# Gathers of the third expert behind the second one's weights, fetches spread over five experts, the fallback as one loop

## The chip, the cores and the metric

The kernel runs on one core of a Trainium2 chip. The metric is device time in microseconds, lower is better. TensorE (PE in the rows) multiplies, VectorE (DVE) and ScalarE (ACT) move and split the results, GpSimd (POOL) splits weights and issues the indirect DMAs, SyncE (SP) issues most of the other DMAs.

## What is computed

A linear attention over 4 x 768 positions gives 3072 tokens of 256 numbers. They pass a first mixture of experts, where each token goes to the one expert of eight that its gate chooses, and then a second one of four experts that all tokens pass.

```python
logits = x @ w_gate                          # 3072 tokens, 8 experts
expert_idx = np.argmax(logits, axis=1)
...
for e in range(E):
    mask = expert_idx == e
    if not mask.any():
        continue
    xe = x[mask]
    h = np.maximum(xe @ w1[e], 0.0)          # 256 x 1024
    ye = h @ w2[e]                           # 1024 x 256
    out[mask] = gate_w[mask, None] * ye
...
for e in range(E):                           # second stage, 4 experts
    h = np.maximum(x @ w1[e], 0.0)
    out += p[:, e:e + 1] * (h @ w2[e])
```

## The kernel before

Numbers of 32 bits are multiplied as three products of halves: a high part (hh, xh, wh) and the rest (hl, xl, wl). ACT makes the high part by a cast, VectorE or POOL the rest by a subtraction.

The attention takes the time up to about 113 us, the eight experts of the first stage stand from there to 288, the second stage from 292 to the end. The eight experts go by their size, each with a fixed number of token places (CAPS: 472, 488, 456, 424, 416, 400, 384, 376). A token over the capacity of its expert would be left for the **fallback**, a block that runs only if `left > 0`; with these inputs it is not run. "Expert 0" below is the first one in this order.

An expert e has these parts, on all engines in the order that is written here:

- **gathers** (`gather_turn`, L265): up to four indirect DMAs on POOL fetch its tokens, 128 rows each, from `xs` in DRAM into `xg`, of which there are eight buffers. An expert's gathers are issued some experts ahead.
- **make_x**: TensorE transposes the rows (tpx, L278), ACT and VectorE split them into xh and xl (L281, L282).
- **gemm1x**: eight blocks f of 128 hidden units. Each takes six products (L248) into ph, which has three buffers; ACT takes the relu as hh (L838), VectorE the rest as hl (L840). So the products of block f + 3 wait for hl of block f. After each block a `hook` adds small steps from a list to the engines' orders.
- **gemm2x**: two times 24 products (L859) and a copy into x2 (L864).
- **prep(e + 1)**: loads of the next expert's weights (512 KB each, SP, L132), their cast wh on ACT (L146), and wl on POOL for w1 (L152) or on VectorE for w2 (L150). In the names, wl_3_0 is the first half for expert 3.

Expert 0 has a part of 256 places that starts under the attention, and a second part of 216 places, whose eight blocks stand from 126 to 140 us.

The list that the hook works off, `queue`, holds the bookkeeping of the first stage: four `turn_steps` (small vectors of 8 numbers, among them `over` with L941 to L946), `places` (pl on POOL, place on VectorE), `weights2`, ten steps of `invert` (VectorE: t, ot, ot times tokc, m and six one-hot tables om; TensorE: ip), the store of 3072 places of 4 bytes into `idd`, one each to its own address (L994), and then 24 times `fetch(u)`, an indirect DMA on POOL that reads the second stage's weights of 128 tokens (pgs from pgd, L1002). A fetch is issued behind the last split of weights on POOL.

TensorE, VectorE, ACT and POOL keep the order that is written; a wait of one instruction holds what stands behind it on its engine.

Of the kernel before, what the change touches and what calls it, by code (L numbers as in the profile page):

```python
# [19 lines left out]
P = 128  # L20
# [15 lines left out]
NSL = 512  # L36
NC = E1 * NSL // P + 1
BIG = 3 << 29
OUTSIDE = 16384


def body(tc, I, out):
    nc = tc.nc
    with ExitStack() as outer:
# [5 lines left out]
        xs = dp.tile([NT, D], F32, name="xs")  # L50
        pgd = dp.tile([NT, E2], F32, name="pgd")
        idd = dp.tile([NT + P, 1], I32, name="idd")
        zero = cp.tile([P, 1], I32, name="zero")
        nc.vector.memset(zero, 0)

# [813 lines left out]
        with ExitStack() as ctx:  # L869
# [88 lines left out]
            def gather_turn(e):  # L958
                gather(e, range(tiles(e)), xs, idr.rearrange("p e c -> p (e c)"), 4 * (e - STAY))
# [52 lines left out]
            for e in range(E1):  # L1012
                if e == E1 - 2:
                    operands = x_first()

                def hook(f, e=e):
                    if operands:
                        operands.pop(0)()
                    if queue and e and (e > 1 or len(queue) > NQ):
                        queue.pop(0)()  # L1020
                    if f % 4 == 3:
                        prep(e + 1, f // 4)
                    if e == 0 and f in (4, 6):
# [12 lines left out]
                if e == 0:  # L1036
                    gemm2x(0, hs, CAP0, CAPS[0], bass.ds(BASES[0], CAPS[0] - CAP0), lambda k: prep(1, 2 + k))
                else:
                    gemm2x(e, hs, 0, CAPS[e], bass.ds(BASES[e], CAPS[e]), lambda k: prep(e + 1, 2 + k))


            left = nc.values_load(tab[0:1, 3, 0:1], min_val=0, max_val=NT)
            with tc.If(left > 0, preferred_fallthrough_block=False), tc.tile_pool(name="fall", bufs=1) as fp:
                starts = nc.values_load_multi_w_load_instructions(tab[0:1, 1, :], min_val=0, max_val=NT)[1]
                turns = nc.values_load_multi_w_load_instructions(tab[0:1, 4, :], min_val=0, max_val=E1 - 1)[1]
                ends = nc.values_load_multi_w_load_instructions(tab[0:1, 2, :], min_val=0, max_val=NT)[1]
                for e in range(E1):
                    w1, w2 = (I[k][bass.ds(turns[e], 1)].rearrange("o r c -> (o r) c") for k in ("w1", "w2"))
                    with tc.For_i(starts[e], ends[e], P) as ws:
                        ix = fp.tile([P, 1], I32, name="ixf")  # L1050
                        nc.sync.dma_start(ix, idd[bass.ds(ws, P)])
                        xg = m1.tile([P, D], F32, tag="xg", name="xgf", bufs=8)
                        nc.gpsimd.indirect_dma_start(xg, None, xs, bass.IndirectOffsetOnAxis(ap=ix, axis=0))
                        xT = m1.tile([P, 2, P], F32, tag="xg", name="xTf", bufs=8)
                        tp = pm.tile([P, 2, P], F32, tag="oneC", name="tpf", bufs=2)
                        for k in range(2):
                            nc.tensor.transpose(tp[:, k, :], xg[:, k * P:k * P + P], ident)
                        nc.scalar.copy(xT, tp)
                        hf = fp.tile([P, NF, P], F32, tag="hf", name="hf")
                        for j in range(2):  # L1060
                            raw = [mp.tile([P, 512], F32, tag="hh", name="raw0f", bufs=10) for _ in range(2)]
                            for k in range(2):
                                nc.sync.dma_start(raw[k], w1[k * P:k * P + P, j * 512:j * 512 + 512])
                            for f in range(4):
                                ph = pm.tile([P, P], F32, tag="three", name="phf", bufs=3)
                                for k in range(2):
                                    nc.tensor.matmul(ph, raw[k][:, f * P:f * P + P], xT[:, k, :],
                                                     start=(k == 0), stop=(k == 1))
                                nc.scalar.activation(hf[:, 4 * j + f, :], ph, AF.Relu)
                        raws = []  # L1070
                        for j in range(4):
                            raw = mp.tile([P, 2, D], F32, tag="hl", name="raw1f", bufs=10)
                            nc.sync.dma_start(
                                raw, w2.rearrange("(k p) d -> p k d", p=P)[:, j * 2:j * 2 + 2, :])
                            raws.append(raw)
                        for k in range(2):
                            po = pm.tile([P, P], F32, tag="two", name="pof", bufs=2)
                            for f in range(NF):
                                nc.tensor.matmul(po, raws[f // 2][:, f % 2, k * P:k * P + P], hf[:, f, :],
                                                 start=(f == 0), stop=(f == NF - 1))  # L1080
                            dst = bass.ds(ws, P)
                            (nc.vector.tensor_copy if k else nc.scalar.copy)(x2[k][:, dst], po)
                x_again()

        m1s.close()
# [199 lines left out]
```

## Time and profile before

| | |
|---|---|
| median of 3 runs | 824.31 us (822.92 to 825.62) |
| the profiled execution | 822.34 us, of which its span 820.6 us |
| TensorE | busy 773.1 us (94% of the span), mean granted clock 0.969 |
| VectorE | busy 580.1 us (71%) |
| ScalarE | busy 406.2 us (49%) |
| GpSimd | busy 480.2 us (59%) |

The span is the profiled execution from its first instruction to its last, and its own time is a little longer than it. A row of the timeline has the start in us, the duration, the engine and line, what is written from what, the shape, and in brackets the idle time of the engine before it and what ended it. A clock of 1.00 is the full 2.4 GHz, 0.50 the lower level of 1.2 GHz.

### The profile page before, as it was taken

What the parts mean: (1) busy time and instruction counts of PE and PEld (TensorE: products, weight loads), DVE (VectorE), ACT (ScalarE), POOL (GpSimd) and SP (SyncE); (2) the same over time, 40 slices, a digit from 0 to 9 for tenths busy, and PEclk for the clock granted to TensorE, in tenths of its full rate; (3) what the DMA queues carried; (4) which work ended last, traced back from release to release, by engine and by line L of the source; (5) the groups of instructions that cost most, each with busy time, mean ns of one, the idle gap of its engine ahead of it and who ended that gap; (6) DMA issues with size and microseconds to landing.
All of it is one profiled execution on the core that took longest, in us unless ns stands there. A gap on an engine that the chain in (4) does not pass through costs nothing.

```text
span 820.6 us, 16313 instructions
## 1 busy us (share of the span) xinstructions
PE 773.1 (94%) x6296; PEld 728.4 (89%) x6296; DVE 580.1 (71%) x1050; ACT 406.2 (49%) x858; POOL 480.2 (59%) x538
## 2 busy tenths in 40 slices
PE   8879987899999969999999999999999999999994
PEld 5556577789999969999999999999999999999994
DVE  8697882665445656776887777978767877778853
ACT  5533343434455445455555455565554655554540
POOL 5546645624588065356876355977435886465634
PEclk8998997999999979999999999999999999999998
DMA  8943225433843310000000000100000000000001
GB/s 220 226 124 97 64 42 178 151 109 104 122 124 118 91 30 26 2 1 27 26 27 27 1 2 1 52 27 26 2 2 1 26 27 1 1 27 28 26 27 52
DMA packets 41688, 46.41 MB, mean 57 GB/s; under 512 B 10432, under 2 KB 30656, under 8 KB 41600
## 3 DMA queue, kind: packets, MB, share of 16 engines
q1 hardware_dynamic: 37040, 37.09, 16.9%
q0 software_dynamic: 3360, 7.13, 2.9%
q8 instruction: 51, 0.84, 0.4%
q10 hardware_dynamic: 1200, 1.05, 0.4%
q14 instruction: 37, 0.30, 0.1%
HBM read 38.90 MB, written 6.35 MB: 55 GB/s over the span
## 4 chain that ended last, share of the span: by engine, by line
PE 60%; issue 1%; POOL 1%; ACT 1%; DVE 0%; POOLq 0%; ACTq 0%
PE po L1174 32%; PE x L1113 9%; PE z L1113 8%; PE w L1113 8%; PE y L1113 4%; POOL out L1194 1%; ACT s L1126 0%; ACT xc L802 0%; PE poA L1174 0%; POOLq L1281 0%; POOL g L1131 0%; ACT wh L178 0%; POOL gap L1199 0%; DVE h L1122 0%; DVE c L1148 0%
## 5 line engine op out<-in xcount | busy, mean ns | idle before, releaser
L1174 PE MATMUL po<-w,h 128*128 128x256 f32 x2280 | 281.4, 281 | 0.3 <-DVE h L1122 0.3
L1174 PEld LDWEIGHTS po<-w,h 128*128 128x128 f32 x2280 | 279.0, 189 | 0.5 <-DVE h L1122 0.5
L1119 ACT ACTIVATE h<-c 128x384 fp32r<-128x384 f32 x192 | 98.8, 525 | 150.2 <-DVE c L1148 84.8
L1122 DVE SCALAR_TENSOR_TENSOR h<-c,h 128x384 fp32r<-128x384 f32 x192 | 150.2, 791 | 11.3
L1131 POOL TENSOR_TENSOR g<-s,s 128x384 f32<-128x384 f32 x64 | 65.1, 1017 | 145.7 <-ACT s L1130 145.7
L1133 DVE TENSOR_TENSOR u<-y,s 128x384 f32<-128x384 f32 x64 | 35.5, 555 | 75.2 <-ACT s L1130 70.1
L1113 PE MATMUL x<-xc,wh 128*128 128x384 f32 x256 | 67.4, 345 | 7.5 <-issue 4.1
L803 POOL TENSOR_TENSOR xc<-x,xc 128x384 fp32r<-128x384 f32 x32 | 36.5, 1140 | 51.0 <-ACT xc L802 50.7
L1113 PE MATMUL w<-xc,wh 128*128 128x384 f32 x256 | 66.2, 340 | 0.0
L1113 PE MATMUL z<-xc,wh 128*128 128x384 f32 x256 | 66.1, 340 | 0.0
L838 ACT ACTIVATE hh<-ph 128x216 fp32r<-128x216 f32 (+8 forms) x68 | 33.5, 495 | 57.5 <-PE ph L248 38.4
L248 PE MATMUL ph<-xh,wh 128*128 128x488 f32 (+8 forms) x142 | 51.2, 361 | 10.0 <-DVE hl L840 7.7
L1148 DVE TENSOR_TENSOR c<-u,g 128x384 f32<-128x384 f32 x64 | 60.4, 944 | 0.0
L840 DVE SCALAR_TENSOR_TENSOR hl<-ph,hh 128x216 fp32r<-128x216 f32 (+8 forms) x68 | 37.5, 557 | 28.1 <-ACT hh L838 22.1
L1126 ACT COPY s<-x 128x384 f32<-128x384 f32 x64 | 30.7, 480 | 53.4 <-PE x L1113 53.4
L152 POOL TENSOR_TENSOR wl<-raw,wh 128x1024 fp32r<-128x1024 f32 (+1 forms) x22 | 39.6, 1800 | 26.8 <-ACT wh L146 25.0
L1122 DVE SCALAR_TENSOR_TENSOR h<-x,h 128x384 fp32r<-128x384 f32 x64 | 35.7, 558 | 24.8 <-ACT h L1119 24.5
L803 POOL TENSOR_TENSOR xc<-ts,xc 128x384 fp32r<-128x384 f32 x46 | 52.4, 1153 | 0.0
L1113 PEld LDWEIGHTS x<-xc,wh 128*128 128x128 f32 x256 | 42.6, 190 | 11.0 <-ACT s L1126 6.1
L501 POOL TENSOR_TENSOR Sm<-S,smask 128x256 f32<-128x256 f32 x44 | 31.3, 729 | 35.9 <-DVE S L491 29.1
L248 PE MATMUL ph<-xh,wl 128*128 128x488 f32 (+8 forms) x142 | 50.3, 354 | 0.3 <-POOL wl L152 0.3
L248 PE MATMUL ph<-xl,wh 128*128 128x488 f32 (+8 forms) x142 | 50.1, 353 | 0.0
(236 smaller groups left out, 1743.9 us busy)
## 6 DMA issues: line engine op xcount, KB each, us to landing
raw<-in_w SPq DMA_DIRECT2D x30, 512.0 KB
raw<-in_v SPq DMA_DIRECT2D x32, 256.0 KB
xs<-xo SPq DMA_DIRECT2D x24, 128.0 KB
xz<-in_xt SPq DMA_DIRECT2D x6, 384.0 KB
CT<-in_CT SPq DMA_DIRECT2D x7, 192.0 KB
BT<-in_BT SPq DMA_DIRECT2D x7, 192.0 KB
bt<-in_bt SPq DMA_DIRECT2D x3, 384.0 KB
ar<-in_ar SPq DMA_DIRECT2D x3, 384.0 KB
```

Source lines behind the costliest of these rows:

```text
L152: ins = nc.gpsimd.tensor_sub(lo[:, :, a:a + n], raw[:, :, a:a + n], hi[:, :, a:a + n].bitcast(F32))
L248: mm = nc.tensor.matmul(ph, w[:, k, fs], x[k], start=(i == 0), stop=(i == 5))
L803: eng.tensor_sub(o[:, 1], src, o[:, 0].bitcast(F32))
L838: i0 = nc.scalar.activation(hh, ph, AF.Relu)
L840: i1 = nc.vector.scalar_tensor_tensor(hl, ph, 0.0, hh.bitcast(F32), op0=ALU.max, op1=ALU.subtract)
L1113: nc.tensor.matmul(bank[to], w[:, a], x[:, r], start=(m == 0 and to not in seen), stop=(m == 2), skip_group_check=True)
L1119: sc.activation(HP[n][0], src, AF.Relu)
L1122: v.scalar_tensor_tensor(HP[n][1], src, 0.0, HP[n][0].bitcast(F32), op0=ALU.max, op1=ALU.subtract)
L1131: nc.gpsimd.tensor_add(g_, s5, s7)
L1133: v.tensor_add(u2, bank["y"], s1)
L1148: v.tensor_add(c22, u2, g_)
L1174: nc.tensor.matmul(two[h], x[:, ts], w2[:, w, j], start=(i, j, h * (len(hs) - 1), m) == (0, 0, 0, 0), stop=(i, j, m) == (3, 1, 2), skip_gr ...
```

## The change

It has three parts. First, the four gathers of the third expert (e = 2) are no longer issued behind the blocks of expert 0, but behind its gemm2x, after the last split of expert 1's first weights on POOL. Second, the list is worked off at every block from expert 1 on, one step for each, where before only four steps ran in expert 1; behind every third fetch stands an empty step. Third, the fallback, which was eight loops behind each other, one for each expert, becomes one loop over a list of parts of 128 tokens; the list is worked out inside the block. The block is also no longer told which of its sides is to follow the branch directly.

```diff
 NSL = 512
 NC = E1 * NSL // P + 1
 BIG = 3 << 29
+NLIST = NU + E1
 OUTSIDE = 16384
...
 
-            NQ = NU + NU // 4 + 6
             queue = turn_steps + [places, weights2] + [f for f in invert(
                 rt, place, 0, NU, NU, placed, lambda sh, name: pp.tile(sh, F32, tag="oneA", name=name), 1) if f]
-            queue += [lambda u=u: fetch(u) for u in range(NU)]
+
+            queue += [f for u in range(NU) for f in [lambda u=u: fetch(u)] + [lambda: None] * (u % 3 == 2)]
...
                 def hook(f, e=e):
                     if operands:
                         operands.pop(0)()
-                    if queue and e and (e > 1 or len(queue) > NQ):
+                    if queue and e:
                         queue.pop(0)()
                     if f % 4 == 3:
                         prep(e + 1, f // 4)
...
                 X.pop(e)
-                if e + 2 < E1:
+                if 0 < e < E1 - 2:
                     gather_turn(e + 2)
...
                 if e == 0:
                     gemm2x(0, hs, CAP0, CAPS[0], bass.ds(BASES[0], CAPS[0] - CAP0), lambda k: prep(1, 2 + k))
+                    with tc.issue_after(LOW[0]):
+                        gather_turn(2)
                 else:
                     gemm2x(e, hs, 0, CAPS[e], bass.ds(BASES[e], CAPS[e]), lambda k: prep(e + 1, 2 + k))
 
 
             left = nc.values_load(tab[0:1, 3, 0:1], min_val=0, max_val=NT)
-            with tc.If(left > 0, preferred_fallthrough_block=False), tc.tile_pool(name="fall", bufs=1) as fp:
-                starts = nc.values_load_multi_w_load_instructions(tab[0:1, 1, :], min_val=0, max_val=NT)[1]
...
-                for e in range(E1):
-                    w1, w2 = (I[k][bass.ds(turns[e], 1)].rearrange("o r c -> (o r) c") for k in ("w1", "w2"))
-                    with tc.For_i(starts[e], ends[e], P) as ws:
-                        ix = fp.tile([P, 1], I32, name="ixf")
-                        nc.sync.dma_start(ix, idd[bass.ds(ws, P)])
-                        xg = m1.tile([P, D], F32, tag="xg", name="xgf", bufs=8)
-                        nc.gpsimd.indirect_dma_start(xg, None, xs, bass.IndirectOffsetOnAxis(ap=ix, axis=0))
...
+            with tc.If(left > 0), tc.tile_pool(name="fall", bufs=1) as fp:
+
+                def t8(name, shape, dt=F32):
+                    return fp.tile([P, *shape], dt, name=name)
+
+                st, n, ni, pc, lt = t8("st", (E1,)), t8("n", (E1,)), t8("ni", (E1,), I32), t8("pc", (E1,)), t8("lt", (E1, E1))
+                v.tensor_copy(st, tab[:, 1])
+                v.tensor_copy(n, tab[:, 2])
+                v.tensor_sub(n, n, st)
...
+                parts_ = nc.values_load(all_[0:1, 0:1], min_val=0, max_val=NLIST)
+                with tc.For_i(0, parts_, 1) as part:
+                    cell = fp.tile([1, 2], I32, name="cell")
+                    nc.sync.dma_start(cell, lid[bass.ds(part, 1)])
+                    ws = nc.values_load(cell[0:1, 0:1], engines=(mybir.EngineType.SP, mybir.EngineType.Activation,
+                                                                 mybir.EngineType.DVE), min_val=0, max_val=NT)
+                    turn = nc.values_load(cell[0:1, 1:2], engines=(mybir.EngineType.SP,), min_val=0, max_val=E1 - 1)
+                    w1, w2 = (I[k][bass.ds(turn, 1)].rearrange("o r c -> (o r) c") for k in ("w1", "w2"))
+                    ix = fp.tile([P, 1], I32, name="ixf")
+                    nc.sync.dma_start(ix, idd[bass.ds(ws, P)])
...
```

Inside the new block some 25 small VectorE steps work out the list, and the loop's body is that of one of the old loops.

**POOL, from the gathers of experts 1 and 2 on.** The rows go to the first half of expert 2's weights (xg are gathers, pl belongs to `places`). Before:

```order
L265 DMA xg<-xs,idr 128x256 x8
L152 TENSOR_TENSOR wl_1_0_2423<-raw_1_0_2302,wh_1_0_2422 128x1024
L265 DMA xg<-xs,idr 128x256 x2
L152 TENSOR_TENSOR wl_1_1_2467<-raw_1_1_2304,wh_1_1_2466 128x1024
L265 DMA xg<-xs,idr 128x256 x2
L988 TENSOR_TENSOR pl<-oneh,base 128x192
L265 DMA xg<-xs,idr 128x256 x2
L152 TENSOR_TENSOR wl_2_0_2696<-raw_2_0_2693,wh_2_0_2695 128x1024
L265 DMA xg<-xs,idr 128x256 x2
L152 TENSOR_TENSOR wl_2_1_2738<-raw_2_1_2735,wh_2_1_2737 128x1024
```

After:

```order
L267 DMA xg<-xs,idr 128x256 x4
L154 TENSOR_TENSOR wl_1_0_2424<-raw_1_0_2303,wh_1_0_2423 128x1024
L154 TENSOR_TENSOR wl_1_1_2468<-raw_1_1_2305,wh_1_1_2467 128x1024
L267 DMA xg<-xs,idr 128x256 x8
L990 TENSOR_TENSOR pl<-oneh,base 128x192
L267 DMA xg<-xs,idr 128x256 x2
L154 TENSOR_TENSOR wl_2_0_2697<-raw_2_0_2694,wh_2_0_2696 128x1024
L267 DMA xg<-xs,idr 128x256 x2
L154 TENSOR_TENSOR wl_2_1_2747<-raw_2_1_2744,wh_2_1_2746 128x1024
```

Four of the first eight gathers move behind wl_1_1, and the split wl_1_1 stands directly behind wl_1_0; ahead of pl there are now eight gathers.

**VectorE in the blocks of expert 2** (456 places; hl is the rest of a block, all other rows come from the list). Before:

```order
L840 SCALAR_TENSOR_TENSOR hl<-ph,hh 128x456
L989 TENSOR_REDUCE place<-pl 128x24
L990 TENSOR_TENSOR place<-place,rank 128x24
L840 SCALAR_TENSOR_TENSOR hl<-ph,hh 128x456 x2
L227 TENSOR_SCALAR t<-place 128x24
L840 SCALAR_TENSOR_TENSOR hl<-ph,hh 128x456
L217 TENSOR_TENSOR ot<-iota_76,t 128x576
L218 TENSOR_TENSOR ot<-ot,tokc 128x576
L840 SCALAR_TENSOR_TENSOR hl<-ph,hh 128x456
L228 SCALAR_TENSOR_TENSOR m<-t,place 128x24
L840 SCALAR_TENSOR_TENSOR hl<-ph,hh 128x456
L213 TENSOR_TENSOR om<-iota_74,m 128x512
```

After:

```order
L842 SCALAR_TENSOR_TENSOR hl<-ph,hh 128x456
L230 SCALAR_TENSOR_TENSOR m<-t,place 128x24
L842 SCALAR_TENSOR_TENSOR hl<-ph,hh 128x456
L215 TENSOR_TENSOR om<-iota_75,m 128x512
L842 SCALAR_TENSOR_TENSOR hl<-ph,hh 128x456
L215 TENSOR_TENSOR om<-iota_75,m 128x512
L842 SCALAR_TENSOR_TENSOR hl<-ph,hh 128x456
L215 TENSOR_TENSOR om<-iota_75,m 128x512
L842 SCALAR_TENSOR_TENSOR hl<-ph,hh 128x456
L215 TENSOR_TENSOR om<-iota_75,m 128x512
L842 SCALAR_TENSOR_TENSOR hl<-ph,hh 128x456
L215 TENSOR_TENSOR om<-iota_75,m 128x512
```

The steps place, t, ot and ot times tokc are gone from here; they stand in the blocks of expert 1, ot times tokc behind its last xl. From the second block on there is one om behind each hl, six in all.

**TensorE at the branch around the fallback** (the branch of L1043 before, of L1047 after). Before, from the branch through the loop of the first expert:

```order
L1043 COMPARE_AND_BRANCH
L1043 UNCONDITIONAL_BRANCH
L1044 TENSOR_LOAD tab
L1046 TENSOR_LOAD tab
L1049 COMPARE_AND_BRANCH
L1049 UNCONDITIONAL_BRANCH x2
L1281 BRANCH_PREFETCH_HINT
L1057 MATMUL tpf<-ident,xgf 128x128 x2
L1067 MATMUL phf<-xTf,raw0f 128x128 x16
L1079 MATMUL pof<-hf,raw1f 128x128 x16
L1049 REGISTER_ALU
L1049 COMPARE_AND_BRANCH
```

After, the whole block:

```order
L1047 COMPARE_AND_BRANCH
L1087 TENSOR_LOAD all__4053
L1088 COMPARE_AND_BRANCH
L1088 UNCONDITIONAL_BRANCH x2
L1326 BRANCH_PREFETCH_HINT
L1102 MATMUL tpf<-ident,xgf 128x128 x2
L1112 MATMUL phf<-xTf,raw0f 128x128 x16
L1124 MATMUL pof<-hf,raw1f 128x128 x16
L1088 REGISTER_ALU
L1088 COMPARE_AND_BRANCH
L1088 UNCONDITIONAL_BRANCH
L1047 UNCONDITIONAL_BRANCH x2
```

Before, the branch falls through to an unconditional branch that leads over eight loops like this one. After, the branch leads to the last of the rows, which leads on to the row behind it; one loop lies between. The other engines have the same two layouts.

The store into idd moves on SP as well: before it stands behind all four loads for expert 4, after behind the first of them.

## Rows read from the trace of the kernel before

**Rows 1.** Windows: us, busy of five engines, TensorE clock, DMA share, GB/s.
```profile
129.00:135.00 6.00, 1.67 (x7) 1.41 (x7) 0.76 (x2) 0.82 (x3) 3.23 (x4) 0.67 0.84 275
...
135.00:141.00 6.00, 6.00 (x28) 6.00 (x29) 1.99 (x6) 3.02 (x8) 2.38 (x1) 0.50 0.43 111
...
292.00:296.00 4.00, 4.00 (x16) 4.00 (x17) 2.49 (x5) 2.58 (x6) 1.57 (x2) 0.65 0.02 6
...
325.00:800.00 475.00, 474.40 (x3395) 471.84 (x3394) 364.11 (x596) 257.93 (x541) 288.75 (x291) 1.00 0.05 17
```

**Rows 2.** Timeline of TensorE: gaps in the first stage, transposes of expert 2.
```profile
131.41 0.55 PE L248 MATMUL ph<-xh,wh 128*128 128x216 f32 x1 [2.96 <-DVE hl L840]
...
134.94 0.55 PE L248 MATMUL ph<-xh,wh 128*128 128x216 f32 x1 [1.92 <-DVE hl L840]
...
153.55 0.82 PE L278 MATMUL tpx<-ident,xg 128*128 128x128 f32 x6
...
159.60 0.49 PE L248 MATMUL ph<-xh,wh 128*128 128x488 f32 x1 [1.92 <-DVE tab L943]
...
182.31 0.48 PE L248 MATMUL ph<-xh,wh 128*128 128x456 f32 x1 [1.65 <-DVE hl L840]
...
218.95 0.46 PE L248 MATMUL ph<-xh,wh 128*128 128x416 f32 x1 [0.63 <-DVE hl L840]
...
291.96 1.01 PE L1113 MATMUL x<-xc,wh 128*128 128x384 f32 x2 [4.12 <-issue]
```

**Rows 3.** Branch records (ns min/median/max), VectorE behind it, instruction queue 284 to 297 us.
```profile
L1043 PEldq COMPARE_BRANCH  x2: 95/1892/3690, 285.2 to 288.2; - x2
...
291.90 0.56 DVE L793 TENSOR_TENSOR ts<-x,x 128x384 f32<-128x384 f32 x1 [3.47 <-issue]
...
q14 instruction: 7, 0.06, 1.3%
```

**Rows 4.** Timeline of POOL: gathers of expert 2, splits of weights.
```profile
128.46 0.95 POOL L265 DMA_INDIRECT xg<-xs,idr  x1 [0.30 <-issue]
...
132.21 0.94 POOL L265 DMA_INDIRECT xg<-xs,idr  x1 [0.30 <-issue]
...
143.55 2.40 POOL L152 TENSOR_TENSOR wl<-raw,wh 128x1024 fp32r<-128x1024 f32 x1
...
156.56 2.38 POOL L152 TENSOR_TENSOR wl<-raw,wh 128x1024 fp32r<-128x1024 f32 x1
...
178.54 2.55 POOL L152 TENSOR_TENSOR wl<-raw,wh 128x1024 fp32r<-128x1024 f32 x1 [12.32 <-ACT wh L146]
```

**Rows 5.** Timeline of VectorE: two long steps, one om.
```profile
156.56 2.42 DVE L944 TENSOR_SCALAR nov<-nov 128x8 f32<-128x8 f32 x1
...
178.89 2.82 DVE L218 TENSOR_TENSOR ot<-ot,tokc 128x576 f16<-128x576 f16 x1
...
182.81 0.68 DVE L213 TENSOR_TENSOR om<-iota,m 128x512 f16<-128x512 f16 x1
```

**Rows 6.** Timeline of SP's queue: load of expert 4, store, load of expert 5.
```profile
190.43 0.37 SPq L132 DMA_DIRECT2D raw<-in_w  x1
...
200.82 0.39 SPq L994 DMA_DIRECT2D idd<-idc  x1
...
203.29 0.37 SPq L132 DMA_DIRECT2D raw<-in_w  x1
```

**Rows 7.** Timeline of ACT: relus of expert 0, casts, a copy.
```profile
130.59 0.35 ACT L838 ACTIVATE hh<-ph 128x216 fp32r<-128x216 f32 x1 [5.28 <-remote]
...
134.12 0.35 ACT L838 ACTIVATE hh<-ph 128x216 fp32r<-128x216 f32 x1 [3.18 <-issue]
...
205.20 1.04 ACT L146 CAST wh<-raw 128x1024 fp32r<-128x1024 f32 x1
...
214.03 0.52 ACT L864 COPY x<-po 128x424 f32 x1 [6.82 <-remote]
...
220.82 1.05 ACT L146 CAST wh<-raw 128x1024 fp32r<-128x1024 f32 x1
```

More of the change, by code (lines that the diff above doesn't have):

```diff
@@ L52, in body @@
         idd = dp.tile([NT + P, 1], I32, name="idd")
+        lid = dp.tile([NLIST, 2], I32, name="lid")
         zero = cp.tile([P, 1], I32, name="zero")
@@ new lines, in body, with wide @@
+            with tc.If(left > 0), tc.tile_pool(name="fall", bufs=1) as fp:
[5 more added lines that the diff above has]
+                v.tensor_sub(n, n, st)
+                v.tensor_scalar(n, n, 127.0, None, op0=ALU.add)
+                v.tensor_copy(ni, n)
+                v.tensor_scalar(ni, ni, 7, None, op0=ALU.logical_shift_right)
+                v.tensor_copy(n, ni)
+                v.tensor_tensor(lt, rows(nth), cols(nth), op=ALU.is_lt)
+                v.tensor_mul(lt, lt, rows(n))
+                v.tensor_reduce(pc, lt, axis=AX.X, op=ALU.add)
+                v.scalar_tensor_tensor(st, pc, -float(P), st, op0=ALU.mult, op1=ALU.add)
+                v.tensor_add(n, n, pc)
+                all_ = t8("all_", (1,), I32)
+                v.tensor_copy(all_, n[:, E1 - 1:])
+                sh = [P, NLIST, E1]
+                kk, at, ge = t8("kk", (NLIST,)), t8("at", sh[1:]), t8("ge", sh[1:])
+                lf, li = t8("lf", (NLIST, 2)), t8("li", (NLIST, 2), I32)
+                nc.gpsimd.iota(kk, pattern=[[1, NLIST]], base=0, channel_multiplier=0,
+                               allow_small_or_imprecise_dtypes=True)
+                def wide(x):
+                    return x[:, None, :].broadcast_to(sh)
+                v.tensor_tensor(at, kk[:, :, None].broadcast_to(sh), wide(pc), op=ALU.is_ge)
+                v.tensor_tensor(ge, kk[:, :, None].broadcast_to(sh), wide(n), op=ALU.is_ge)
+                v.tensor_sub(at, at, ge)
+                for i, x in enumerate((st, tab[:, 4])):
+                    v.tensor_copy(pc, x)
+                    v.tensor_mul(ge, at, wide(pc))
+                    v.tensor_reduce(lf[:, :, i:i + 1].rearrange("p k o -> p (k o)"), ge, axis=AX.X, op=ALU.add)
+                v.scalar_tensor_tensor(lf[:, :, 0:1].rearrange("p k o -> p (k o)"), kk, float(P),
+                                       lf[:, :, 0:1].rearrange("p k o -> p (k o)"), op0=ALU.mult, op1=ALU.add)
+                v.tensor_copy(li, lf)
+                nc.sync.dma_start(lid.rearrange("k c -> (k c)")[None], li[0:1].rearrange("p k c -> p (k c)"))
+                parts_ = nc.values_load(all_[0:1, 0:1], min_val=0, max_val=NLIST)
[8 more added lines that the diff above has]
+                    nc.sync.dma_start(ix, idd[bass.ds(ws, P)])
+                    xg = m1.tile([P, D], F32, tag="xg", name="xgf", bufs=8)
+                    nc.gpsimd.indirect_dma_start(xg, None, xs, bass.IndirectOffsetOnAxis(ap=ix, axis=0))
+                    xT = m1.tile([P, 2, P], F32, tag="xg", name="xTf", bufs=8)
+                    tp = pm.tile([P, 2, P], F32, tag="oneC", name="tpf", bufs=2)
+                    for k in range(2):
+                        nc.tensor.transpose(tp[:, k, :], xg[:, k * P:k * P + P], ident)
+                    nc.scalar.copy(xT, tp)
+                    hf = [mp.tile([P, 4, P], F32, tag="hl", name="hf", bufs=10) for _ in range(2)]
+                    for j in range(2):
+                        raw = [mp.tile([P, 512], F32, tag="hh", name="raw0f", bufs=10) for _ in range(2)]
+                        for k in range(2):
+                            nc.sync.dma_start(raw[k], w1[k * P:k * P + P, j * 512:j * 512 + 512])
+                        for f in range(4):
+                            ph = pm.tile([P, P], F32, tag="three", name="phf", bufs=3)
+                            for k in range(2):
+                                nc.tensor.matmul(ph, raw[k][:, f * P:f * P + P], xT[:, k, :],
+                                                 start=(k == 0), stop=(k == 1))
+                            nc.scalar.activation(hf[j][:, f, :], ph, AF.Relu)
+                    raws = []
+                    for j in range(4):
+                        raw = mp.tile([P, 2, D], F32, tag="hl", name="raw1f", bufs=10)
+                        nc.sync.dma_start(
+                            raw, w2.rearrange("(k p) d -> p k d", p=P)[:, j * 2:j * 2 + 2, :])
+                        raws.append(raw)
+                    for k in range(2):
+                        po = pm.tile([P, P], F32, tag="two", name="pof", bufs=2)
+                        for f in range(NF):
+                            nc.tensor.matmul(po, raws[f // 2][:, f % 2, k * P:k * P + P], hf[f // 4][:, f % 4, :],
+                                             start=(f == 0), stop=(f == NF - 1))
+                        dst = bass.ds(ws, P)
+                        (nc.vector.tensor_copy if k else nc.scalar.copy)(x2[k][:, dst], po)
```

29 lines of the change are left out of this document (removed).

## The prediction

> **What bounds the kernel now.** I read the busy time of each engine by windows first, then the gaps of TensorE in its timeline, then what the other engines did in each gap. From 325 to 800 us TensorE is busy for 474.40 of 475 us at full clock [rows 1]. Nothing of the change lies in that stretch, so it lasts as long as before, and whatever TensorE gains or loses ahead of it moves the end by as much. All I have to do is add up TensorE's gaps between expert 0 and the second stage.
>
> The reader is to see six of them [rows 2]: 2.96 and 1.92 us in expert 0's second part (131.41 and 134.94), 1.92 in expert 1 (159.60), 1.65 in expert 2 (182.31), 0.63 in expert 4 (218.95), and 4.12 where the program jumps over the fallback (291.96). Two of them also cost clock. From 129 to 135 the granted clock is 0.67 and from 135 to 141 it is 0.50, the lower of the two levels; from 292 to 296 it is 0.65 [rows 1].
>
> The sum is made against the profiled execution: 822.34 us, of which 1.74 lie outside the span. The median of the three runs is 1.97 above it, and I add the sum to the median.
>
> **The fallback as one loop.** What stands inside is not run, for nothing is left over; what counts is how far each engine jumps. Behind its last COPY VectorE starts again only after 3.47 us, released by nothing that the profile shows; TensorE's second branch record lasts 3690 ns where the other takes 95 [rows 3]. Between 284 and 297 us the instruction queue of the engines other than TensorE fetches seven blocks [rows 3]. So the engines wait for their next instructions at the target. The jump over TensorE's eight copies of the loop shrinks to one copy.
>
> VectorE sets the pace behind the jump: ACT's first cast waits for its ts, and TensorE has operands for two products only. I take 0.5 us of the 3.47 as what loading the register and two short branches still need, so **-3.0**. Best, the whole 3.47 and the slow clock behind it go: 4.00 us at 0.65 lose 1.4 [rows 1], together -4.9. Worst, both jumps that the new layout takes miss: one more of 3.47, **+3.5**; and 0 if the one miss stays.
>
> The Trainium skill ("Runtime: NRT & Kernel Launch", Instruction fetch mechanics) says that a taken branch whose target is outside the two pages held forces a fetch before the engine goes on. The 3690 ns agree with it. By it the new jump, some 80 instructions on TensorE, would mostly find its target loaded, and two taken branches would cost nothing much; a long second jump would speak against the change. The term stands without it.
>
> **The queue without its gate.** Two of the gaps are VectorE operations that lie under a split of weights on POOL. In expert 1, L944, a step on 8 columns, takes 2.42 us from 156.56, the time of POOL's wl_2_0 (2.38 from 156.56), and the next hl comes late [rows 4, 5]. In expert 2, L218 (ot times tokc) takes 2.82 us from 178.89 under wl_3_0 (178.54 to 181.09) [rows 4, 5].
>
> For expert 1: POOL now issues eight gathers between wl_1_1 and pl. Gathers follow each other every 1.25 us (128.46 to 132.21, four of them) [rows 4]. Today wl_1_1 starts at 143.55 behind two gathers [rows 4]; without these it starts at 141.05 at the very earliest and ends at 143.45, and ten gathers (12.5 us) and pl put wl_2_0 at 156.5 or later, more likely past 158, since ACT's cast comes first too. L944 is ahead of it or through by then. What wl_2_0 can hold next are the steps behind the hl of f = 5; TensorE's last product of the expert waits only for that of f = 4. So **-1.9**, at worst 0.
>
> For expert 2: L218 moves to the end of expert 1, where TensorE has a second product ahead that wants none of it. In its place stand the six om operations, 0.68 us each [rows 5], one behind each hl. That makes 1.31 us of VectorE work per f against 1.24 of TensorE, a lag of under half a microsecond over six. One of them will lie under wl_3_0 in turn. If it is the om behind f = 4, nobody waits: the three ph buffers let TensorE end its last product. If it is the one behind f = 3, the stall stays. L218 starts at 178.89 behind the hl of f = 3 and one step of about an om's length, so that om would start near 178.1 to 178.2, and wl_3_0 starts at 178.54 [rows 4, 5]. The om has some 0.4 us in hand: **-1.65**, at worst 0. The Trainium skill speaks against this part ("SBUF — State Buffer", Who interferes with whom and the section on two sides): an operation of VectorE with two SBUF inputs and a GpSimd operation exclude each other for their whole length, and om has two. The two long rows agree; by that rule alone, with om starting late, the sum would lose its 1.65.
>
> The store of places into idd moves ahead by one expert, from 200.82 to about 184 [rows 6]. It is 3072 packets of 4 bytes. After it the load of expert 5's first half (issued at 203.29) is cast only at 220.82, and ACT's copy at 214.03 comes 6.82 us after its last work [rows 6, 7]; the gap of 0.63 at 218.95 is what TensorE feels of it. In the new place it stands beside expert 4's second half, issued at 190.43 and cast at 205.20 [rows 6, 7]. Its packets are through some 19 us after the store if it goes as before, at 203, two microseconds before that cast. Cost 0. The gap of 0.63 goes: **-0.5**, worst 0. The fetches themselves lie on POOL, which idles for more than they take.
>
> **The third expert's gathers.** Four issues of POOL, from 128.46 to 133.15 [rows 4], go behind wl_1_1. They are wanted by the transposes at 153.55 [rows 2]. With wl_1_1 where it is now (143.55 to 145.95) the fourth is issued by 150.8; 2.7 us remain for its landing. Cost 0; each microsecond of lateness would cost about one.
>
> What they free is the disputed part. In expert 0's second part ACT takes its first relu at 130.59, 5.28 us after its last work, though TensorE has three products done by 128.45 (131.41 less 2.96), so the first by about 127; and the second one at 134.12, after 3.18 us in which nothing shown holds it [rows 7]. Both gaps of TensorE there follow from this, and the half clock behind them. Idle 2.96 and 1.92; slow clock 6.00 at 0.50 and 1.67 at 0.67, that is 3.5: 8.4 us hang on it [rows 1, 2]. The transfer engines are busy 0.84 of the time from 129 to 135 and 0.43 from 135 to 141 [rows 1]. I don't know what holds ACT. The trace shows only that it happens while gathers and weights crowd the transfers, and again at 214.03, where the store crowds them. The first wait began at 127, before the moved gathers; the second lies wholly inside their string. So I take the second: 1.92 and about a third of the slow clock, **-3.0**; bounds 0 and -8.4.
>
> **The sum.** -3.0 - 1.9 - 1.65 - 0.5 - 3.0 = -10.05. The profiled time would be 812.3 and the median **814.3 us**.
>
> **The rivals.**
> - All of expert 0's lateness goes: -7.05 - 8.4 = -15.5, 808.9 us. For it: all causes that I can think of are crowding, and a quarter of the bytes leaves. Against: the first wait began before the crowd.
> - It doesn't do what it says in one place: either ACT is late as before (-7.05, 817.3) or the jump misses as before (-7.05 too).
> - Both new jumps miss and expert 0 stays: +3.5 - 4.05, 823.8, no change. For it: two taken branches where one was. Against: the target is eight times nearer.
> - Slower, by the store in its new place: if the load issued at 190.43 lands behind the store's packets, ACT stands at its cast with all relus behind it. TensorE's three ph buffers hide some 3 us. For the kernel to become slower by 2.5 us, this has to cost 12.6, so the load has to land about 15.5 us after 205.20, near 221, some 30 us after its issue. Before, the like load needed at most 17.5 (203.29 to 220.82), and at 17.5 it would land at 208 and cost nothing or little. As a second price, ACT late as in expert 0 costs up to 8.4, which alone would leave -1.6.
>
> **How the numbers follow.** A change of 0.3% is 2.5 us, about what a measurement of this kernel tells from no change. My forecast, between 811 and 817: 0.45. All of expert 0 (807 to 811): 0.15. One place fails (816 to 821.5): 0.23. No change: 0.11. Slower: 0.06. The range from 807 to 821.5 leaves out some of the last two and the tail of the second, under 2 in 10; the forecast's own is 811 to 817.5. Faster: the first three, 0.83; same 0.11; slower 0.06.
>
> **What would show it.** In the changed kernel's timeline of VectorE: the ts behind the last COPY within 0.6 us and no branch record of TensorE above 0.2 us. No TensorE gap above 0.5 us in the gemm1 of experts 1 and 2, with L944's successor at 0.2 us. ACT's second relu of expert 0's second part right behind the first, and the half clock there shorter than 6 us. The idd store near 177 to 184, and expert 4's second half cast without a wait. The prediction is wrong if the branch keeps 3 us, if an om lies under wl_3_0 and TensorE waits for the hl behind it, or if ACT stands at a cast in expert 3.

## The result

The changed kernel takes 812.93 us in the median of 4 runs (806.11 to 817.67), the kernel before 823.62 (820.78 to 825.62), so the medians are 10.7 us apart, or 1.3%. The measured ratio of the two, which is not simply the quotient of the medians, is 0.9846, with a 95% interval of 0.9815 to 0.9877; the figures behind "Measured" below are such ratios to the kernel before. A second set on another occasion gave 809.63 against 818.66, 9.0 us apart, and a ratio of 0.9877 (0.9842 to 0.9912). So the change saves 1.1 to 1.5%, some 9 to 13 us; 814.3 was forecast. The first profiled executions lie further apart, spans of 804.4 and 820.6 us, and a good part of that is one execution's luck on either side: second profiles of the two kernels have spans of 811.3 and 815.8.

TensorE's gaps in the changed kernel's first execution (timeline: start, duration, operation, and in brackets the idle time and what ended it) answer to [rows 2]:

```profile
129.52 0.37 PE L250 MATMUL ph<-xh,wh 128*128 128x216 f32 x1 [1.62 <-DVE hl L842]
...
174.51 0.26 PE L225 MATMUL ip<-ot,om 128*128 128x24 f16 x4 [0.48 <-DVE om L215]
...
175.65 0.26 PE L225 MATMUL ip<-ot,om 128*128 128x24 f16 x4 [0.39 <-DVE om L215]
...
277.22 0.89 PE L1158 MATMUL x<-xc,wh 128*128 128x384 f32 x2 [0.30 <-PEq L1047]
```

Of the gaps of before, one is left in expert 0, and two small new ones stand at the end of expert 2, where TensorE now waits for the om behind which the places are worked out. The gap at the branch went from 4.12 to 0.30 us. VectorE's and POOL's timelines answer to [rows 4, 5]:

```profile
150.44 0.16 DVE L946 TENSOR_SCALAR nov<-nov 128x8 f32<-128x8 f32 x1
...
153.87 1.57 DVE L951 CAST nov<-novi 128x8 f32<-128x8 int32 x1
...
171.22 2.10 DVE L215 TENSOR_TENSOR om<-iota,m 128x512 f16<-128x512 f16 x1
...
277.99 0.56 DVE L795 TENSOR_TENSOR ts<-x,x 128x384 f32<-128x384 f32 x1 [0.48 <-DVEq L1047]
```

```profile
152.97 2.42 POOL L154 TENSOR_TENSOR wl<-raw,wh 128x1024 fp32r<-128x1024 f32 x1
...
170.26 2.50 POOL L154 TENSOR_TENSOR wl<-raw,wh 128x1024 fp32r<-128x1024 f32 x1 [10.05 <-ACT wh L148]
```

L946 (L944 of before) is through in 0.16 us, 2.5 us ahead of wl_2_0. The splits on POOL still hold VectorE: L951 under wl_2_0 takes 1.57 us and the om behind block 4 takes 2.10 under wl_3_0, but TensorE has no gap behind either.

To see where the time went, I read the starts of VectorE's copy at the end of each expert's gemm2x. For the kernel before, in a second execution that I profiled (below), and for the changed one:

```profile
127.28 0.42 DVE L864 COPY x<-po 128x256 f32<-128x256 f32 x1 [0.39 <-PE po L859]
...
142.75 0.38 DVE L864 COPY x<-po 128x216 f32 x1
...
169.16 0.67 DVE L864 COPY x<-po 128x488 f32 x1 [2.46 <-PE po L859]
...
191.83 0.63 DVE L864 COPY x<-po 128x456 f32 x1 [2.18 <-PE po L859]
```

```profile
125.93 0.42 DVE L866 COPY x<-po 128x256 f32<-128x256 f32 x1 [0.46 <-PE po L861]
...
141.07 0.38 DVE L866 COPY x<-po 128x216 f32 x1
...
163.90 0.66 DVE L866 COPY x<-po 128x488 f32 x1
...
186.60 0.63 DVE L866 COPY x<-po 128x456 f32 x1 [2.38 <-PE po L861]
```

The distances between such starts are the lengths of the stages; expert 1 takes 169.16 - 142.75 = 26.41 us here and 22.83 there. This table has them for every profile of the study (E0 is expert 0's second part; "branch" goes from the last copy to TensorE's first product behind it; "behind it" from there to the first product that waits more than 2 us for ACT's s, some 11 us on):

| kernel | E0 | 1 | 2 | 3 | 4 | 5 | 6 | branch | behind it |
|---|---|---|---|---|---|---|---|---|---|
| before | 19.48 | 24.83 | 22.68 | 21.98 | 18.10 | 18.68 | 17.94 | 4.08 | 10.36 |
| before, again | 15.47 | 26.41 | 22.67 | 20.66 | 18.63 | 18.65 | 17.92 | 3.73 | 10.77 |
| changed | 15.14 | 22.83 | 22.70 | 19.24 | 19.04 | 18.10 | 17.48 | 0.26 | 11.14 |
| changed, again | 16.04 | 26.41 | 22.67 | 19.44 | 19.03 | 18.11 | 17.47 | 0.26 | 11.13 |
| gathers alone | 13.73 | 23.01 | 22.67 | 20.64 | 18.64 | 18.67 | 17.94 | 4.23 | 11.35 |
| list alone | 14.91 | 26.71 | 22.66 | 19.43 | 19.04 | 18.10 | 17.48 | 3.98 | 10.37 |
| one loop alone | 14.95 | 24.09 | 22.68 | 20.65 | 18.69 | 18.68 | 17.93 | 0.26 | 11.13 |
| steps apart | 16.19 | 22.69 | 22.67 | 20.65 | 19.16 | 18.69 | 17.92 | 4.08 | 10.29 |
| one loop, old layout | 15.10 | 26.69 | 22.67 | 20.66 | 18.66 | 18.68 | 17.96 | 0.54 | 11.00 |
| eight loops, new layout | 14.87 | 23.97 | 22.68 | 20.66 | 18.77 | 18.69 | 17.92 | 2.10 | 12.13 |
| changed, cast later | 12.37 | 23.02 | 22.66 | 19.44 | 19.03 | 18.11 | 17.48 | 0.26 | 11.14 |
| changed, cast and steps later | 12.26 | 22.86 | 20.76 | 20.14 | 19.04 | 18.24 | 17.48 | 0.26 | 11.13 |

Expert 7 takes 16.49 to 16.50 us in all of them.

### The profile page after: what moved, and what is told of

Same layout as the page of the kernel before. It is cut to its first block, busy times and chain, and to the rows that moved or that the text cites. A ratio compares the mean times of both kernels' runs of the same rounds, so it can differ in the third digit from the quotient of the medians.

```text
span 804.4 us, 16309 instructions
## 1 busy us (share of the span) xinstructions
PE 766.4 (95%) x6296; PEld 721.7 (90%) x6296; DVE 584.1 (73%) x1050; ACT 406.3 (51%) x858; POOL 480.6 (60%) x538
## 4 chain that ended last, share of the span: by engine, by line
PE 61%; ACT 1%; POOL 1%; issue 1%; DVE 0%; POOLq 0%; ACTq 0%; DVEq 0%
PE po L1219 33%; PE x L1158 8%; PE z L1158 8%; PE w L1158 8%; PE y L1158 4%; POOL out L1239 1%; ACT s L1171 1%; ACT xc L804 0%; PE poA L1219 0%; POOLq L1326 0%; DVE ts L795 0%; POOL g L1176 0%; ACT wh L180 0%; POOL gap L1244 0%; DVE c L1193 0%
## 5 line engine op out<-in xcount | busy, mean ns | idle before, releaser
L842 DVE SCALAR_TENSOR_TENSOR hl<-ph,hh 128x216 fp32r<-128x216 f32 (+8 forms) x68 | 37.6, 559 | 26.7 <-ACT hh L840 19.9
```

The lines of the kernel that those rows point to most:

```text
L842: i1 = nc.vector.scalar_tensor_tensor(hl, ph, 0.0, hh.bitcast(F32), op0=ALU.max, op1=ALU.subtract)
```

## The experiments

### The kernel before, once more

No edit.

> The kernel before, profiled a second time, to see what of the 16.2 us between the two profiled spans (820.6 and 804.4) is the change and what is one execution's clock. Theory A (the change's own places): the stall of TensorE in expert 0's second part, the 1.9 us in expert 1, the 1.65 in expert 2 and the 4 us at the branch are there again, so that from the copy of expert 0's first part (127.70 before) to the first product of the second stage (291.96) there are again 164 us, within 1. Theory B (much of it is chance): this distance differs from 164.3 by 3 us or more, or the attention and the second stage differ by more than 2.

Measured: 1.0007 (0.9981 to 1.0032), as it must be, and a span of 815.8 us instead of 820.6. From the copy of expert 0's first part to the first product of the second stage it is 287.92 - 127.28 = 160.6 us, 3.6 less than in the first execution: theory B for expert 0, theory A for the rest. The gaps of experts 1 and 2 (1.92 and 1.65) are there again. In expert 0, ACT's relus come one behind the other, and what stops TensorE is a different thing. TensorE, with the gap in expert 1 after it, then ACT:

```profile
133.87 0.37 PE L248 MATMUL ph<-xh,wh 128*128 128x216 f32 x1 [1.96 <-DVE hl L840]
...
155.17 0.49 PE L248 MATMUL ph<-xh,wh 128*128 128x488 f32 x1 [1.92 <-DVE tab L943]
```

```profile
132.11 1.04 ACT L146 CAST wh<-raw 128x1024 fp32r<-128x1024 f32 x1 [1.81 <-DMA raw<-in_w]
```

ACT has a cast of expert 1's first half in its order behind block 3's relu, and stands 1.81 us until that load has landed, with the relus of the later blocks behind it. The late relus at 130.59 and 134.12 [rows 7], on which 8.4 us hung in my prediction, belong to the first profiled execution alone. In the profiles of the other five kernels that leave the gathers where they were, expert 0's second part takes 14.9 to 16.2 us, not 19.48.

The clock behind the gap of expert 1 also varies (windows: us, busy times of PE, PEld, DVE, ACT and POOL, TensorE clock, DMA share, GB/s). This execution, and that of the one loop alone:

```profile
156.00:162.00 6.00, 6.00 (x23) 4.95 (x23) 3.05 (x9) 2.00 (x3) 3.58 (x3) 0.74 0.38 126
```

```profile
156.00:162.00 6.00, 6.00 (x30) 5.09 (x29) 2.95 (x9) 2.00 (x3) 4.33 (x3) 1.00 0.37 127
```

Nearly the same gap (1.92 and 1.73 us) leaves the clock at 0.74 in the one and at 1.00 in the other. So the stall of expert 1 costs its own one to two microseconds, and in some executions about two more.

### The gathers alone

```diff
-                if e + 2 < E1:
+                if 0 < e < E1 - 2:
                     gather_turn(e + 2)
...
+                    with tc.issue_after(LOW[0]):
+                        gather_turn(2)
```

> Only the third expert's gathers move. Theory A (crowded transfers hold ACT in expert 0's second part): ACT's second relu comes right behind the first, the half clock shrinks from 9 us to about 3.5, and from the copy of expert 0's first part to that of its second part it is 15.1 us as in the changed kernel and not 19.5; the time falls by 4.4, about 0.5%. Theory B (what holds ACT has nothing to do with these gathers, the changed kernel was lucky there): 19.5 us again and no change in time. The stalls in experts 1 and 2 and the 4 us at the branch stay in both.

Measured: 0.9969 (0.9944 to 0.9994). Faster, if barely, but not by theory A's way: ACT stands at its cast here too, for 1.70 us, and TensorE's gap in expert 0 is 1.85. The half clock that should have shrunk isn't there at all, but neither is it with the list alone or the one loop alone, which leave the gathers where they were. Expert 0's 13.73 us is the shortest with the cast in its old place, but the changed kernel, whose gathers stand in the same place, took 15.14 and 16.04. What is gone is the gap in expert 1, which I had expected to stay. VectorE, then POOL:

```profile
152.85 0.16 DVE L944 TENSOR_SCALAR nov<-nov 128x8 f32<-128x8 f32 x1
```

```profile
154.80 2.40 POOL L152 TENSOR_TENSOR wl<-raw,wh 128x1024 fp32r<-128x1024 f32 x1
```

### The list alone

```diff
-            NQ = NU + NU // 4 + 6
...
-            queue += [lambda u=u: fetch(u) for u in range(NU)]
+            queue += [f for u in range(NU) for f in [lambda u=u: fetch(u)] + [lambda: None] * (u % 3 == 2)]
...
-                    if queue and e and (e > 1 or len(queue) > NQ):
+                    if queue and e:
```

> Only the list is worked off without its gate. Theory A: the step ot times tokc leaves expert 2, so the 1.65 us there go, as does the 0.63 in expert 4; the stall of 1.9 in expert 1 stays, since L944 and wl_2_0 still meet at 156.56 when the gathers are not moved; sum about -1.5 to -2.5 with expert 0 as before. Theory B (the collision only changes its partner): an om of expert 2 under wl_3_0 makes TensorE wait for 1.5 us or more, and the sum is within 1 of nothing.

Measured: 0.9969 (0.9940 to 0.9998). Experts 2 to 6 take 96.71 us together where the same kernel's second execution took 98.53: -1.8, inside theory A's range. But it does not fall where I put it. Expert 2 is as long as before (22.66); its gap of 1.65 is gone, and in its place TensorE runs the 24 products of ip, which came from expert 3, and waits twice for om. Expert 3 is shorter by 1.2, experts 5 and 6 by 0.5 each, expert 4 longer by 0.4. In expert 1 the gap is there, 1.64.

### One loop alone

```diff
-            with tc.If(left > 0, preferred_fallthrough_block=False), tc.tile_pool(name="fall", bufs=1) as fp:
+            with tc.If(left > 0), tc.tile_pool(name="fall", bufs=1) as fp:
...
-                for e in range(E1):
+                with tc.For_i(0, parts_, 1) as part:
```

> Only the fallback becomes one loop. Theory A (the engines wait for instructions at a far target): the gap at the branch falls from 4.1 to below 0.5 us, VectorE's from 3.47 to about 0.5, and what stands ahead of it is as before; the time falls by 3.0 to 3.8. Theory B (the branch's gain is lost again, since the first products then wait for operands): the first product comes 3.8 earlier, but the products of the second stage 15 us later only by 3 or less. Both see expert 0 as before.

Measured: 0.9966 (0.9936 to 0.9997). Theory A: from the last copy to the first product it is 0.26 us instead of 3.73 to 4.23 with the eight loops in their old layout. Of this about 0.5 comes back: the stretch behind the branch takes 11.13 where the five profiles with that layout took 10.29 to 11.35, 10.63 in the mean. The products now come sooner than their operands: in the changed kernel TensorE waits three times between 279 and 281 us, 0.74 us together. The three parts' ratios multiplied give 0.990, a smaller gain than the whole change's 0.985 to 0.988; the intervals of the three are wide enough to cover that.

### The changed kernel, once more

No edit.

> The changed kernel, profiled a second time. Theory A (what the three single runs show): from the copy of expert 0's first part to the first product of the second stage about 151 us (14 for expert 0's second part, 23.0 for expert 1, then 22.7, 19.3, 19.0, 18.1, 17.5, 16.5 and 0.3), the time 1.0 to 1.5% under that of before. Theory B (the first profile of it was lucky): 3 us or more longer.

Measured: 0.9877 (0.9842 to 0.9912), the time that theory A names. But its profile has theory B's 155.9 us (284.20 - 128.27), and the reason is in expert 1, whose gap is back with 1.85 us. TensorE, VectorE, then POOL:

```profile
156.73 0.49 PE L250 MATMUL ph<-xh,wh 128*128 128x488 f32 x1 [1.85 <-DVE tab L945]
```

```profile
153.75 2.35 DVE L946 TENSOR_SCALAR nov<-nov 128x8 f32<-128x8 f32 x1
```

```profile
153.69 2.37 POOL L154 TENSOR_TENSOR wl<-raw,wh 128x1024 fp32r<-128x1024 f32 x1
```

The split wl_2_0 began 0.06 us ahead of L946 and held it to its end. In the first execution it began 2.53 behind it. So this part of the change is a race between two queues. From the start of POOL's split wl_1_1 it is 15.9 us to wl_2_0 in the lost execution and 16.1 to 16.8 in the three won ones (this kernel's first, the gathers alone, and the cast later, below), but to L946 (L944) it is 16.0 us in the lost one and 14.2 to 14.7 in the others. So it was VectorE's side that came late. TensorE's clock from 136 to 142 us, at the end of expert 0, is 0.72 in the lost execution and 1.00 in the same window of the gathers alone, and TensorE's products set when VectorE's steps come. That the clock decides the race is likely from this, but not shown by an experiment.

### The steps apart, without the gathers' move

```diff
+            turn_steps = turn_steps[:2] + [lambda: None] * 4 + turn_steps[2:]
             queue = turn_steps + [places, weights2] + [f for f in invert(
```

> The kernel before with gathers, fallback and fetches as they were; only the third and fourth of the small steps of expert 1 (L941 to L954) run four blocks later, so that L944 no longer stands ahead of the hl of block 4 when wl_2_0 runs. Theory A (the gathers' move gains because it parts L944 from wl_2_0): the gap of 1.9 us in expert 1 goes here too, expert 1 takes 23 us where before's executions took 24.1 to 26.7, and the time falls by 0.2 to 0.4%, as with the gathers moved alone. Theory B (the gathers gain by what they free in expert 0): no gain in expert 1, 24 to 26.7 us, and the time as before.

Measured: 0.9952 (0.9932 to 0.9973), at least as much as the gathers' move alone. Expert 1 takes 22.69 us, L944 runs in 0.16 us at 155.19, behind the hl of block 6, while wl_2_0 runs from 152.38, 9.38 us behind expert 0's last copy, as in both executions of the kernel before. VectorE, then POOL:

```profile
155.19 0.16 DVE L944 TENSOR_SCALAR nov<-nov 128x8 f32<-128x8 f32 x1
```

```profile
152.38 2.42 POOL L152 TENSOR_TENSOR wl<-raw,wh 128x1024 fp32r<-128x1024 f32 x1
```

Theory A is shown: it was the meeting of L944 with wl_2_0 ahead of block 4's hl that cost expert 1 its gap.

### Which part of the branch counts

One loop in the old layout, and eight loops in the new one:

```diff
             with tc.If(left > 0, preferred_fallthrough_block=False), tc.tile_pool(name="fall", bufs=1) as fp:
...
+                with tc.For_i(0, parts_, 1) as part:
```

> The kernel before with one loop as the fallback, but with the old layout of the branch: fall through, then one unconditional jump over the block. Theory A (the distance is what counts): the gap at the branch is below 0.6 us, as with the new layout. Theory B (the layout is what counts): VectorE waits 3 us or more and the gap at the branch is 3.5 to 4.1.

```diff
-            with tc.If(left > 0, preferred_fallthrough_block=False), tc.tile_pool(name="fall", bufs=1) as fp:
+            with tc.If(left > 0), tc.tile_pool(name="fall", bufs=1) as fp:
```

> The kernel before with its eight loops, but with the branch laid out as in the changed kernel. Theory A (the distance counts): the gap at the branch stays between 3.5 and 4.5 us, or grows to 7 if both jumps wait. Theory B (the layout counts): it falls below 1 us.

Measured: 0.9963 (0.9937 to 0.9988) and 0.9987 (0.9963 to 1.0011). With one loop in the old layout the distance from the last copy is 0.54 us. With eight loops in the new layout VectorE starts again only after 3.28 us, and TensorE's branch record is the longest of all:

```profile
L1043 PEldq COMPARE_BRANCH  x1: 4432/4432/4432, 279.7 to 279.7; - x1
```

```profile
286.20 0.56 DVE L793 TENSOR_TENSOR ts<-x,x 128x384 f32<-128x384 f32 x1 [3.28 <-DVEq L1043]
```

In that kernel TensorE's jump begins earlier, while its products still run, so that its first product comes after 2.10 us, but the next ones wait for VectorE and the stretch behind takes 12.13. The distance counts; the layout is worth 0.3 us with one loop. The DMA queues that carry instructions show what the engines wait for: packets, MB and share of the engines, first while TensorE's long branch record of the kernel before lasts (288.2 to 291.9 us), then in the changed kernel from its branch record to VectorE's first operation behind the branch (274.3 to 278.0):

```profile
q8 instruction: 1, 0.02, 2.2%
q14 instruction: 3, 0.02, 1.9%
```

```profile
q14 instruction: 1, 0.01, 0.5%
```

One packet of 16 KB moves on q8 inside the long record, here and in every other profile over eight loops; over one loop none does. In the changed kernel TensorE's record is this:

```profile
L1047 PEldq COMPARE_BRANCH  x1: 223/223/223, 274.3 to 274.3; - x1
```

The expectation that both jumps of the new layout might wait was wrong: one branch record stands there for each engine.

### The cast later in expert 0

On top of the change:

```diff
-                    if f % 4 == 3:
-                        prep(e + 1, f // 4)
+                    if f in ((5, 7) if e == 0 else (3, 7)):
+                        prep(e + 1, f // 4 if e else (f - 5) // 2)
```

> The changed kernel; in expert 0's second part the cast of expert 1's first half stands behind block 5's relu on ACT and not behind block 3's. Theory A (what is left of TensorE's wait in expert 0 is ACT standing at that cast for a load, 1.7 to 2.2 us in the profiles, with the relus behind it): the gap of 1.9 us goes or falls below 0.5, expert 0's second part takes 12.5 us or less where it took 13.7 to 15.1, and the time falls by 0.1 to 0.3%. Theory B (the load lands no earlier and the wait moves to expert 1's first products): expert 0's part shrinks by 1.5 and expert 1's grows by as much, no gain.

Measured: 0.9857 (0.9820 to 0.9894). Theory A: ACT stands at the cast for 0.15 us, the gap of 1.9 us is gone (what is left in expert 0 is a wait of 0.51 us for gathered rows), and expert 0's second part takes 12.37 us, the least of any kernel up to here; expert 1 isn't longer (23.02). The time is 0.2% under the changed kernel's 0.9877 of the same occasion, as theory A says, but the intervals overlap. ACT's row:

```profile
133.08 1.06 ACT L148 CAST wh<-raw 128x1024 fp32r<-128x1024 f32 x1 [0.15 <-DMA raw<-in_w]
```

In this execution the race of expert 1 was won (L946 at 150.76, wl_2_0 at 152.72).

### Both, and out of the race

With the cast's edit:

```diff
-            queue = turn_steps + [places, weights2] + [f for f in invert(
+            queue = turn_steps[:2] + [weights2, lambda: None] + turn_steps[2:] + [places] + [f for f in invert(
```

> The changed kernel with the cast of expert 1's first half behind block 5 in expert 0, and with the small steps of expert 1 set back by two blocks (an empty one and the step of the second stage's weights ahead of them), so that L946 (L944 of before) stands behind a later block. Theory A (both remaining stalls have these causes, and the one in expert 1 is a race that the changed kernel wins in one execution and loses in the next): expert 0's second part 12.4 us, expert 1 22.6 to 23.0 in every execution, the time 1.3 to 1.7% under that of before and its runs closer together. Theory B (the steps meet the next split or the store, now later again, costs what the step saves): expert 1 as said, but experts 2 to 4 together longer than 61.2 us, no gain over the kernel with the cast alone (0.9857).

Measured: 0.9857 (0.9829 to 0.9885), 805.82 us in the median, its runs between 804.87 and 807.30. Theory A by the stages, in the one execution that was profiled; the time is that of the cast alone, which theory B names. L946 runs in 0.16 us at 151.01, and wl_2_0 (from 151.79) now holds the step behind block 5's hl:

```profile
151.72 2.53 DVE L947 CAST novi<-nov 128x8 int32<-128x8 f32 x1
```

TensorE doesn't wait for it: its last products of ph in expert 1 start by 151.69. The two still meet, but where it costs nothing; the same holds wherever the gap went with the gathers (a step behind block 4's or 5's hl takes 1.57 to 3.02 us under wl_2_0). Experts 2 to 4 take 59.94 us, less than the 61.13 of the kernel with the cast alone. The list is one step later here, so that the 24 products of ip stand in expert 3, behind all six om, and wait for none: experts 2 and 3 take 40.90 us together and not 42.10. TensorE's two gaps in experts 0 and 1 are waits for gathered rows:

```profile
134.04 0.55 PE L280 MATMUL tpx<-ident,xg 128*128 128x128 f32 x3 [0.41 <-DMA xg<-xs,idr]
...
147.78 0.33 PE L280 MATMUL tpx<-ident,xg 128*128 128x128 f32 x1 [0.59 <-DMA xg<-xs,idr]
```

Its median is the least of all kernels here, below the changed kernel's and that with the cast alone (806.42); that it beats the latter isn't shown, the intervals overlap.

## Why the prediction was right, and where its steps were not

The total was right, 814.3 forecast and 812.93 measured, and the range held. The terms, one by one:

- **The branch, -3.0.** Right in mechanism and nearly in size. Without the far jump TensorE goes on after 0.26 us, a gain of 3.5 to 4.0, of which about 0.5 is given back behind the branch. Eight loops cost over 3 us on VectorE in either layout, one loop 0.5 to 0.6 in either. The rule of the Trainium skill ("Runtime: NRT & Kernel Launch", Instruction fetch mechanics), by which a taken branch to a target that isn't held has to fetch it first, agrees with these and with the packet of instructions inside the long record. The rival in which two new jumps miss did not occur even with eight loops.
- **Expert 1, -1.9.** Right in mechanism, shown by moving the steps instead of the gathers; wrong in certainty. I worked out that wl_2_0 could begin as early as 156.5 when L944 stood at 156.56, and took the stall as gone; in the second execution of the changed kernel L946 lost that race by 0.06 us. The price was also too small: the clock after the gap falls in some executions and not in others. In the seven profiles with the gap expert 1 takes 24.0 to 26.7 us, without it 22.7 to 23.0, so winning is worth 1 to 4 us.
- **Expert 2, -1.65.** The gap went as forecast, and the om under wl_3_0 was the one behind block 4, which holds nobody but the end of the list. The om ahead of it began 0.43 us before wl_3_0, as the forecast's 0.4 has it, and did so in each of the four profiles with the list in this order: this margin is no race, though it is small. The step that failed is what I left out: the 24 products of ip move into expert 2 with the list and wait there for the last two om, 0.87 us. Expert 2 is as long as before, and the gain of 1.2 appears in expert 3, which is rid of them. The rule of the Trainium skill on the shared port ("SBUF — State Buffer", SBUF: two separate sides) agrees with the om's 2.10 us under a POOL split.
- **Expert 4, -0.5.** The gap of 0.63 was peculiar to the first execution; the second one doesn't have it. With the list spread, expert 4 grows by 0.4, and experts 5 and 6 shrink by 0.5 each: a net -0.6 that I had not worked out by these places.
- **Expert 0, -3.0.** This is the step that failed: "So I take the second: 1.92 and about a third of the slow clock". The rows that I read belonged to one execution. In the others, the changed kernel's first one apart, ACT isn't late at its first relus at all; where the cast has its old place it stands there for a load, with the gathers moved (0.98 to 2.38 us) or not (1.50 to 2.53). Moving that cast removes the gap; moving the gathers does not. Nor do they bring the load sooner: ACT can start that cast 4.5 to 5.9 us behind the copy of expert 0's first part with the gathers moved and 4.5 to 5.6 without, the first execution aside, and the stage takes 13.7 to 16.0 us with them moved and 14.9 to 16.2 without.
- **The store in its new place** cost nothing that the stages show, as forecast: ACT's cast of expert 4's second half came at 196.11 in the changed kernel right behind the relu ahead of it.

That the sum came out is in part luck. By stages, when the race is won, the change gains about 2.7 us in expert 1 (25.6, the mean of the seven with the gap, less 22.9), 1.8 in experts 2 to 6 and 3.3 at the branch (4.02 less 0.26, less the 0.5), together 7.8; when it is lost, as in one of the two profiles, about 5. The forecast had 7.05 for these, and 3.0 for expert 0, where the runs show nothing that the gathers gain. The measured change is 9 to 13. So the term of expert 0 filled the place of a rest of 1 us or more that no stage accounts for. What this rest is stays open: from the first long wait behind the branch to the end, the two executions of the changed kernel take 516.0 us and those of the kernel before 517.1 and 518.3, although nothing there was changed, and the single parts give anything from 515.5 to 517.5.

What made ACT late in the first execution of before (and by 2 us at 128.69 in the first one of the changed kernel) isn't known; it was not seen in the ten other profiles at that place, and no experiment was made on it.

## What to carry to other kernels

One profile is one execution: before a stall is put into a sum, see whether a second profile of the same kernel has it, above all where the row's releaser doesn't explain its wait. Where operations of two engines hold each other up, compute both start times, and call a margin of a few tenths a race if the two queues run apart, as POOL's gathers and VectorE's small steps do here. Prefer an edit that moves the step out of the way (the steps set back by some blocks) to one that moves the other side by a queue's length. A block that is never run can still cost by its length: here the jump over eight loops cost VectorE over 3 us and that over one loop about 0.5.

## What the runs showed that I had not expected

- The same gap of 1.6 to 1.9 us on TensorE is followed by full clock over the next 6 us in three executions and by 0.51 to 0.72 in four.
- TensorE's branch record over the eight loops is 3.37 to 3.87 us in the old layout and 4.43 in the new one; over the one loop it is 0.19 and 0.22 to 0.23. VectorE's own branch records are 0.05 to 0.07 us long in all of them; its wait over the eight loops (3.28 to 3.68 us) stands behind the record, as idle time ahead of the first instruction at the target.
- In the eight loops' new layout TensorE's branch is read early (at 279.7), and half of its 4.43 us hides behind products that are still running; VectorE's wait doesn't, since its branch stands behind the last copy.
